# Two pairs of the first batch in two rounded parts from row 256 on, with the first expert unit's product grown chunk by chunk

## The chip, the cores and the metric

The kernel runs on one core of one Trainium2 chip. The metric is the device time of one execution in microseconds (us), as the median of several runs.

The engines are named as in the profile: PE is TensorE (matrix products), PEld its weight loads, DVE is VectorE, ACT is ScalarE, POOL is GpSimd, SP is SyncE, which here only issues DMAs.

## The reference

Inputs: q, k, v of 4 batches x 8 heads x 576 rows x 64, a forget gate f per row, and two pairs of weights (512 x 2048 and 2048 x 512). The output has 2304 rows of 512.

```python
scores = scale * np.matmul(q, k.transpose(0, 1, 3, 2))
cum = np.cumsum(np.log(np.clip(f, 0.0001, 1.0)), axis=-1)
decay = cum[:, :, :, None] - cum[:, :, None, :]
scores = np.where(causal, -1000000000.0, scores + decay)
attn = softmax(scores)                    # over the last axis
x = np.matmul(attn, v)                    # heads side by side: 2304 x 512
h = x @ w_in;  x = np.maximum(h, 0.0) ** 2 @ w_out
h = x @ w2_in; out = np.where(h > 0, h, np.exp(np.minimum(h, 0)) - 1) @ w2_out
```

## The kernel before, in words

**Attention** takes the heads of a batch in pairs, four pairs to a batch. A head's rows come in two parts: part A is rows 0 to 255, part B rows 256 to 511; step 4 takes the last 64 rows of both heads of a pair together. In the first batch all four pairs do part A first (8 steps), and then pair by pair step 4 and two B steps (12 steps); the other batches go pair by pair through all five. A step computes scores on PE (`s`), the row minimum on DVE, the exponential on ACT, transposes the result on PE (`pt`), copies it out of PSUM, and multiplies with v on PE (`pv`). A pair's output is scaled (`r`, `rb`, `pr`) and split for what follows (`xs`, or for the first 256 rows of the first batch `x0`).

**Two ways to multiply.** A head can be *plain*: q, k and v stay 32-bit floats (`rawA`, `rawB`, `rawC`, `vp`), a score is one matmul (L374), and the product with v is one (L453); the profile shows two records for each. Or it is in *two rounded parts*: `load_head` makes of the fetched `raw` a rounded part and the rest (`qk1`, `qk2`, `vv`), a score is two single-record matmuls (L378, L379), and the weights are split into two parts as well (`p`, `ptA`, `ptB`), so that v takes two matmuls (L456). Making the parts takes two ACT copies, one DVE cast and four POOL instructions for a head of the first batch's B part, whose lists `ENG` give the engine of each. In the first batch every part A is plain, and part B of all pairs below `PLAIN_B`, which is 4.

**The first expert layer** begins inside attention: six units of 256 rows multiply with the half of the weights that stays on the chip. A unit runs through `ph` (rows times w_in, four banks `fp` of two columns `fc`, 12 matmuls for each `fc`, 3 for each of its four chunks `c` of 128 inputs), `relu2` (ACT, then a square on ACT or POOL, a rounded copy on ACT and the rest `gl` on POOL), and `o` (times w_out, 96 matmuls). A unit is cut into steps of 12 matmuls. At each place in attention the loop adds credit, `PACE` of the batch times the `COST` of the attention step, and spends it on unit steps. The first unit may start when part A of all four pairs of the first batch is stored. Until then `fill()` has PE multiply zeros (`busy`, tile `idle`).

**Expert weights** come as 64-bit words and are made into floats by `words` (L152 on ACT, L153 to L156 on DVE) and then split (L172 on ACT, L121 on DVE); 16 of them are due in the first batch, at the steps that `W_AT` names. Three of their staging buffers are also the buffers of `qk2`.

A scheduler sets the order of the instructions on each engine from the program's order, from the dependences and from costs of its own; each engine then runs its list in order. The DMAs all go through SP's list.

Of the kernel before, what the change touches and what calls it, by code (L numbers as in the profile page):

```python
# [10 lines left out]
F32 = mybir.dt.float32  # L11
# [8 lines left out]
NC = DM // 128  # L20
# [6 lines left out]
CH = 256  # L27
# [3 lines left out]

W_MIN = float(np.uint32(0x38000000).view(np.float32))
W_MAX = float(np.uint32(0x47EFFE00).view(np.float32))
PACE = (1.4, 0.9, 1.85, 1.75)
COST = {'A': 0.7, '4': 1.1, 'B': 1.7}
W_AT = (1, 1, 1, 1, 0, 0, 0, 0, 2, 2, 2, 2, 2, 2)
AHEAD = 2
# [4 lines left out]

PLAIN = (0,)

PLAIN_B = 4
CP = {'pA': 'a', 'pB': 'av', 'xA': 'a', 'xB': 'a'}
ENG = {'qk': 'aav', 'ql': 'ppp', 'kh': 'pvd', 'kl': 'ppp', 'vh': 'ppp', 'vl': 'ppp', 'xl': 'pv'}
NORM = 'ap'
# [23 lines left out]
def f32(ap):  # L72
    return ap.bitcast(F32)
# [10 lines left out]
def attention_then_moe_kernel(ctx, tc, first, firstv, plain, qkv, aug0, f, w1, w2, out):  # L84
    nc = tc.nc
    PS = bass.MemoryType.PSUM

    def pool(stack, name, bufs, side, **kw):
        return stack.enter_context(tc.tile_pool(name=name, bufs=bufs, side=side, reuse_waits="tile", **kw))
# [25 lines left out]
    trail = []  # L115
# [59 lines left out]
    def win(m, fc, part_, c):  # L175
        return wslot[m, fc][:, part_, c * 128:(c + 1) * 128]

    def wout(m, fc, part_, c=None):
        o = wslot[m, fc][:, part_, 512:1024]
        return o if c is None else o[:, c * 128:(c + 1) * 128]  # L180

    def mm3(dst, pairs, first, last, skip=False):
        n = len(pairs)
        for i, (l, r) in enumerate(pairs):
            nc.tensor.matmul(out=dst, lhsT=l, rhs=r, start=first and i == 0,  # L185
                             stop=last and i == n - 1, skip_group_check=skip)

    def three(hl, hr):
        return [(hl[0], hr[0]), (hl[1], hr[0]), (hl[0], hr[1])]
# [10 lines left out]
    ps_o = pool(un, "ps_o", 1, "left", space=PS)  # L200
    ps_h = pool(un, "ps_h", 1, "left", space=PS)
# [4 lines left out]
    x0 = xa.tile([128, 2 * NC, CH], F32R, tag="xu", name="x0")  # L206
# [44 lines left out]
    zero = const.tile([128, 128], F32R, name="zero")  # L251
    nc.vector.memset(f32(zero), 0.0)
    idle = ps_h.tile([128, 512], F32, tag="h", name="idle")

    def busy(n):
        for _ in range(n):
            nc.tensor.matmul(out=idle[:, 0:256].rearrange("p (a b) -> p a b", a=2), lhsT=zero, rhs=zero.unsqueeze(1).broadcast_to([128, 2, 128]), start=True, stop=True)

    busy(WARM)

    raws = {}
# [3 lines left out]
    def fetch_head(b, h, part):  # L265
        if b in PLAIN and (part == "A" or h // 2 < PLAIN_B):
            fetch_plain(b, h, part)
            return
        raw = ab.tile([128, ALL], F32, tag="raw", name="raw", bufs=BUFS["raw"])
        raws[b, h, part] = raw  # L270
        nc.sync.dma_start(out=raw, in_=qkv[b, h])
# [361 lines left out]
    def load_x1(t0, n, pool):  # L633
        x = pool.tile([128, 2 * NC, n], F32R, tag="xu", name="xu")
        for c in range(NC):
            for off, step, b, s in runs(t0, n):
                nc.sync.dma_start(out=f32(x[:, c::NC, off:off + step]), in_=x1[b][c::NC, :, s:s + step].rearrange("c p t -> p c t"))
        return x

    more = {}  # L640

    def unit(u):
        x = load_x1(u * CH, CH, xa) if u else x0
        if not u:
            nc.sync.dma_start(out=x1[0][:, :, 0:CH].rearrange("c p t -> p c t"), in_=f32(x0))
        yield
        gs = []
        for fp in range(4):
            if more and fp % 2:
                ph = more["h"].tile([128, 512], F32, tag="H", name="ph")  # L650
            else:
                ph = ps_h.tile([128, 512], F32, tag="h", name="ph")
            for i in range(2):
                fc = 2 * fp + i
                for c in range(NC):
                    mm3(ph[:, i * CH:(i + 1) * CH], three([win(1, fc, t, c) for t in range(2)], [x[:, c, :], x[:, NC + c, :]]),
                        c == 0, c == NC - 1)
                if i == 0:
                    yield
            gs += [[t[:, i * CH:(i + 1) * CH] for t in ht] for ht in [relu2(ph, 512, GL[0], SQ[fp])] for i in range(2)]  # L660
            yield
        for cp in range(2):
            if more:
                po = more["o"].tile([128, 512], F32, tag=f"O{cp}", name="o").rearrange("p (c t) -> p c t", c=2)
            else:
                po = ps_o.tile([128, 2, CH], F32, tag="o", name="o")
            for fc in range(8):
                for i in range(2):
                    mm3(po[:, i, :], three([wout(1, fc, t, 2 * cp + i) for t in range(2)], gs[fc]), fc == 0 and i == 0, fc == 7, True)
                if fc % 2:  # L670
                    yield
            o = xa.tile([128, 2, CH], F32, tag="o", name="o")
            if CPO == "v":
                nc.vector.tensor_copy(o, po)
            else:
                nc.scalar.activation(out=o, in_=po, func=AF.Copy)
            nc.sync.dma_start(out=part[u][:, 2 * cp:2 * cp + 2, :], in_=o)
        yield

    def drain(gen):  # L680
        for _ in gen:
            pass
# [39 lines left out]
    def ready(u):  # L722
        b, s = divmod(u * CH + CH - 1, S)
        return stored[b] == 2 * (H // 2) or (b in SPLIT and s < 256 and stored[b] >= H // 2)

    stored = [0] * B
    units = [unit(u) for u in range(NU)]
    started = [False] * NU
    wl = weights(1, w1, wa, range(8), False, True)

    wait = [0]
    n_step = [0]

    def moe_step():
        for u in range(NU):
            if units[u] is None:
                continue
            if not started[u] and not ready(u):
                return False
            if not started[u] and u:  # L740
                if wait[0] < DELAY:
                    wait[0] += 1
                    return False
            started[u] = True
            wait[0] = 0
            n_step[0] += 1
            if n_step[0] == 9:
                drain(wl)
            if HOLD is not None and len(trail) > HOLD:
                with tc.issue_after(trail[-1 - HOLD].ins):  # L750
                    left = next(units[u], "end") != "end"
            else:
                left = next(units[u], "end") != "end"
            if left:
                return True
            units[u] = None
        return False

    credit = 0.0
    for i in range(len(todo) + LAG):  # L760
# [12 lines left out]
        if i < len(todo):  # L773
            sg = soft(*todo[i])
            b, hp, kind, k = todo[i]
        else:
            sg = iter(())
        if i >= LAG:
            o = todo[i - LAG]
            og = outs(*o)  # L780
        else:
            o, og = None, iter(())
        for _ in range(W_AT[i] if i < len(W_AT) else 0):
            next(wl, None)
        n_moe = PACE[b] * COST[kind]
        n_out = {"A": 3, "4": 1, "B": 8}[o[2]] if o else 1
# [52 lines left out]
    while moe_step():  # L839
        pass  # L840
# [358 lines left out]
```

## Time and profile before

| | |
|---|---|
| median of 3 runs | 1034.13 us (1031.56 to 1039.54) |
| the profiled execution | 1034.08 us, of which its span 1032.3 us |
| granted TensorE clock | 0.998 of full speed |
| busy over the span | PE 98%, DVE 69%, ACT 51%, POOL 25% |
| attention | 0 to about 362 us; the rest is the two expert layers |

A row of the timeline gives the start and the length of an instruction or of a run of equal ones; lengths of matmuls overlap, since PE is pipelined, so that the distance of two starts is what one costs PE. The chain that ended last gives lengths that don't overlap.

### The profile page before, as it was taken

How to read it: one execution, taken by the hardware profiler on the slowest of the kernel's cores; microseconds unless marked ns; L12 is line 12 of the kernel's file. 1: busy time of each engine (PE TensorE's matmuls, PEld its weight loads, DVE VectorE, ACT ScalarE, POOL GpSimd, SP SyncE). 2: the span in 40 equal slices, each digit the busy share in tenths (PEclk: the TensorE clock that was granted, in tenths of full speed). 3: DMA queues.
4: the chain of work that ended last, by engine and by line, in shares of the span. 5: the costliest groups of instructions: out<-in, count | busy, mean ns of one | idle time of the engine just before them, and what ended most of it. 6: DMA issues, size and time to landing. Idle time of an engine off the chain costs nothing.

```text
span 1032.3 us, 17606 instructions
## 1 busy us (share of the span) xinstructions
PE 1015.1 (98%) x6385; PEld 901.1 (87%) x6385; DVE 707.2 (69%) x1585; ACT 523.1 (51%) x1195; POOL 258.9 (25%) x280
## 2 busy tenths in 40 slices
PE   8999999999999999999999999999999999999998
PEld 7677798999999998889988888888989898899997
DVE  6994588776685548946385779795555999654554
ACT  5774586766676634424253445463334665433331
POOL 2235588576775300003104040300000000000000
PEclk9999999999999999999999999999999999999999
DMA  6764555554641174333545545644415465453402
GB/s 221 220 204 130 185 165 156 184 164 142 182 130 54 45 249 125 128 123 144 168 138 204 201 166 204 225 153 154 136 49 178 145 209 180 126 177 126 147 21 82
DMA packets 73862, 158.47 MB, mean 154 GB/s; under 512 B 9296, under 2 KB 34640, under 8 KB 73744
## 3 DMA queue, kind: packets, MB, share of 16 engines
q1 hardware_dynamic: 73776, 157.36, 46.9%
q8 instruction: 50, 0.82, 0.3%
q14 instruction: 36, 0.29, 0.1%
HBM read 115.15 MB, written 39.22 MB: 150 GB/s over the span
## 4 chain that ended last, share of the span: by engine, by line
PE 93%; DMA 2%; DVE 2%; SPq 1%; POOL 1%; issue 0%; ACT 0%; DVEq 0%; ACTq 0%; POOLq 0%
PE O L185 32%; PE P L185 18%; PE pH L185 13%; PE ph L185 7%; PE o L185 7%; PE pt L449 5%; PE pv L456 4%; PE s L374 2%; PE pv L453 2%; PE s L378 2%; PE s L379 2%; SPq L281 1%; DMA rawB<-in_qkv_dram 1%; DMA wraw<-in_w_dram 1%; PE pr L449 1%; DMA aug<-in_aug_dram 1%
## 5 line engine op out<-in xcount | busy, mean ns | idle before, releaser
L185 PEld LDWEIGHTS P<-xu,v 128*128 128x128 f32 x1536 | 200.5, 189 | 10.8 <-issue 0.6
L185 PE MATMUL P<-xu,v 128*128 128x256 f32 x1536 | 203.8, 282 | 0.4 <-ACT hs L1040 0.4
L185 PE MATMUL O<-v,gh 128*128 128x512 f32 x576 | 169.2, 393 | 1.8 <-ACT gh L1011 1.8
L185 PE MATMUL pH<-xu,w 128*128 128x512 f32 (+1 forms) x672 | 140.8, 360 | 0.0
L185 PEld LDWEIGHTS pH<-xu,w 128*128 128x128 f32 x672 | 114.0, 188 | 20.2
L185 PE MATMUL O<-gh,w 128*128 128x512 f32 (+1 forms) x448 | 122.6, 362 | 0.0
L185 PEld LDWEIGHTS O<-v,gh 128*128 128x128 f32 x576 | 102.9, 188 | 19.7 <-ACT gh L1011 2.0
L185 PE MATMUL O<-v,gl 128*128 128x512 f32 x288 | 100.9, 393 | 0.0
L185 PEld LDWEIGHTS O<-gh,w 128*128 128x128 f32 x448 | 79.8, 189 | 14.1
L1040 ACT ACTIVATE hs<-P 128x256 f32<-128x256 f32 x128 | 48.1, 381 | 81.9 <-PE P L185 81.3
L134 POOL TENSOR_TENSOR yl<-pr,yh 128x512 fp32r<-128x512 f32 x18 | 25.0, 1389 | 250.8 <-ACT yh L860 171.7
L134 POOL TENSOR_TENSOR qk<-raw,qk 64x704 fp32r<-64x704 f32 (+1 forms) x48 | 76.8, 1601 | 22.3 <-DVE qk L129 10.3
L1043 DVE TENSOR_TENSOR hs<-P,hs 128x256 f32<-128x256 f32 x96 | 40.6, 424 | 59.3 <-PE P L185 57.4
L185 PE MATMUL O<-gl,w 128*128 128x512 f32 (+1 forms) x224 | 80.1, 363 | 0.0
L185 PE MATMUL o<-gh,w 128*128 128x256 f32 x384 | 75.8, 290 | 0.0
L1065 ACT ACTIVATE g<-g 128x512 f32<-128x512 f32 x64 | 40.2, 629 | 54.1 <-DVE g L1057 32.2
L152 ACT ACTIVATE wt<-wraw 128x512 f32<-128x512 f32 x57 | 38.4, 675 | 57.4 <-DMA wraw<-in_w_dram 43.1
L618 ACT ACTIVATE gh<-g 128x512 fp32r<-128x512 f32 (+1 forms) x80 | 46.8, 585 | 38.3 <-DVE g L617 35.2
L185 PE MATMUL ph<-xu,w 128*128 128x256 f32 x480 | 65.8, 287 | 0.2 <-ACT g L613 0.2
L617 DVE TENSOR_TENSOR g<-g 128x512 f32<-128x512 f32 (+1 forms) x56 | 45.4, 812 | 26.5 <-ACT g L613 26.3
L1011 ACT ACTIVATE gh<-g 128x512 fp32r<-128x512 f32 x72 | 45.5, 631 | 35.8 <-DVE g L1066 28.8
L185 PEld LDWEIGHTS O<-v,gl 128*128 128x128 f32 x288 | 52.8, 188 | 9.9
(156 smaller groups left out, 2070.2 us busy)
## 6 DMA issues: line engine op xcount, KB each, us to landing
xu<-x SPq DMA_DIRECT2D x66, 512.0 KB
wraw<-in_w_dram SPq DMA_DIRECT2D x57, 512.0 KB
raw<-in_qkv_dram SPq DMA_DIRECT2D x24, 800.0 KB
x<-yh SPq DMA_DIRECT2D x31, 256.0 KB
x<-yl SPq DMA_DIRECT2D x31, 256.0 KB
x<-xs SPq DMA_DIRECT2D x16, 320.0 KB
xu<-x SPq DMA_DIRECT2D x16, 256.0 KB
raws_w<-in_w_dram SPq DMA_DIRECT2D x7, 512.0 KB
```

The costliest lines, as they stand in the source:

```text
L134: nc.gpsimd.tensor_tensor(out=dst, in0=x, in1=f32(hi), op=ALU.subtract)
L152: nc.scalar.activation(out=f32(t), in_=f32(hi), func=AF.Abs)
L185: nc.tensor.matmul(out=dst, lhsT=l, rhs=r, start=first and i == 0, stop=last and i == n - 1, skip_group_check=skip)
L374: seen[0] = nc.tensor.matmul(out=dst, lhsT=hh.t[0:68, hh.q + q0:hh.q + q0 + 128], rhs=hh.t[0:68, hh.k + j0:hh.k + j0 + n], start=first, st ...
L449: seen[0] = nc.tensor.transpose(dst, src, ident[:, c0:c0 + 128])
L456: seen[0] = nc.tensor.matmul(out=dst, lhsT=hh[2][:, J, :], rhs=hl[i], start=first and i == 0, stop=last and i == 1)
L617: (nc.vector if sq == "v" else nc.gpsimd).tensor_tensor(out=g[:, 0:n], in0=g[:, 0:n], in1=g[:, 0:n], op=ALU.mult)
L618: nc.scalar.activation(out=gh[:, 0:n], in_=g[:, 0:n], func=AF.Copy)
L1011: nc.scalar.activation(out=gh, in_=g, func=AF.Copy)
L1040: nc.scalar.activation(out=o, in_=x, func=AF.Copy)
L1043: nc.vector.tensor_tensor(o, y, x, op=ALU.add)
L1065: nc.scalar.activation(out=gs[i], in_=gs[i], func=AF.Exp)
```

## The change

Three things are changed. `PLAIN_B` goes from 4 to 2, so part B and step 4 of the third and the fourth pair of the first batch (heads 4 to 7) go in two rounded parts. The first unit's products for `fp` 0 and 1 are no longer two whole steps each: `begin` computes chunk `c` of both banks when part A of pair `c` is stored, for the first three chunks (six steps of 6 matmuls); the unit itself adds the fourth chunk. The two banks are then open at the same time, one in `ps_h` and one in `ps_o`, and the zero products go into the open bank `ph` and add nothing to it. And `PACE` of the first batch goes from 1.4 to 1.0, with the step at which the remaining weights are drained moved from 9 to 7, since the unit has two steps less.

```diff
-PACE = (1.4, 0.9, 1.85, 1.75)
+PACE = (1.0, 0.9, 1.85, 1.75)
...
-PLAIN_B = 4
+PLAIN_B = 2
...
+    begun = []
+
     def busy(n):
         for _ in range(n):
-            nc.tensor.matmul(out=idle[:, 0:256].rearrange("p (a b) -> p a b", a=2), lhsT=zero, rhs=zero.unsqueeze(1).broadcast_to([128, 2, 128]), start=True, stop=True)
+            out = (begun[0] if begun else idle)[:, 0:256].rearrange("p (a b) -> p a b", a=2)
+            nc.tensor.matmul(out=out, lhsT=zero, rhs=zero.unsqueeze(1).broadcast_to([128, 2, 128]), start=not begun,
+                             stop=not begun, skip_group_check=bool(begun))
...
+    def grow(fp, cs):
+        ph = begun[fp]
+        for c in cs:
+            for i in range(2):
+                mm3(ph[:, i * CH:(i + 1) * CH], three([win(1, 2 * fp + i, t, c) for t in range(2)], [x0[:, c, :], x0[:, NC + c, :]]),
+                    c == 0 and i == 0, c == NC - 1 and i == 1, True)
+
+    def begin():
+        for c in range(NC - 1):
+            for fp in range(2):
+                while stored[0] <= c:
+                    yield False
+                if c == 0:
+                    begun.append((ps_o if fp else ps_h).tile([128, 512], F32, tag="o" if fp else "h", name="ph"))
+                grow(fp, (c,))
+                yield True
...
         for fp in range(4):
-            if more and fp % 2:
+            if not u and fp < 2:
+                ph = begun[fp]
+                grow(fp, (NC - 1,))
+            elif more and fp % 2:
                 ph = more["h"].tile([128, 512], F32, tag="H", name="ph")
             else:
                 ph = ps_h.tile([128, 512], F32, tag="h", name="ph")
             for i in range(2):
+                if not u and fp < 2:
+                    break
...
+    early = begin()
+
     def moe_step():
+        if not started[0]:
+            with tc.issue_after(trail[-1].ins):
+                went = next(early, None)
+            if went is not None:
+                return went
...
-            if n_step[0] == 9:
+            if n_step[0] == 7:
                 drain(wl)
```

How the order moves is shown at three places. In these lists a name stands with the number that its tile has in that program, L260, L378, L382, L383, L453, L457, L460 and L478 of the changed kernel are L257, L374, L378, L379, L449, L453, L456 and L474 of the one before, and `x_122` is `x0`.

**PE, where part A of the third pair is done**, before the first scores from row 256 on. Before:

```order
L453 MATMUL pv<-ea,rawA 64x128
L257 MATMUL idle<-zero 128x256 x14
L374 MATMUL s<-rawA 128x256 x2
L449 MATMUL pt<-ident,e_1_135 128x128 x3
L374 MATMUL s<-rawA 128x256 x2
L449 MATMUL pr<-ident,rb 128x128 x2
```

After:

```order
L260 MATMUL idle<-zero 128x256 x2
L378 MATMUL s<-rawA 128x256 x2
L453 MATMUL pt<-ident,e_1_135 128x128 x3
L185 MATMUL ph<-x_122,w_0_252 128x256 x2
L185 MATMUL ph<-x_122,w_2_315 128x256
L378 MATMUL s<-rawA 128x256 x2
...
L185 MATMUL ph<-x_122,w_1_274 128x256 x3
L260 MATMUL ph<-zero 128x256 x9
```

The first chunk of the unit's product (12 matmuls) now stands here; the second and third stand behind the first scores from row 256 on, and zero products stand beside them.

**PE, at the first scores of the third pair from row 256 on** (`qk_850` to `qk_904` are the parts of its two heads). Before:

```order
L185 MATMUL ph<-x_122,w_5_565 128x256 x3
L449 MATMUL pt<-ident,e_1_135 128x128
L449 MATMUL pt<-ident,eb 128x128 x2
L374 MATMUL s<-rawB 128x288
L374 MATMUL s<-rawC 128x288
L374 MATMUL s<-rawB 128x288
L374 MATMUL s<-rawC 128x288
L453 MATMUL pv<-pp,rawB 64x320
```

After:

```order
L260 MATMUL ph<-zero 128x256 x2
L185 MATMUL ph<-x_122,w_0_252 128x256 x3
L185 MATMUL ph<-x_122,w_1_274 128x256 x3
...
L185 MATMUL ph<-x_122,w_3_375 128x256 x3
L382 MATMUL s<-qk_850 128x288 x2
L383 MATMUL s<-qk_851 128x288
L382 MATMUL s<-qk_903 128x288
L383 MATMUL s<-qk_851 128x288
L382 MATMUL s<-qk_903 128x288
```

The scores are now single-record matmuls on the prepared parts, and the unit has come to `fc` 3 here, where it had come to `fc` 5.

**POOL, from the end of part A of the first batch on.** Before:

```order
L134 TENSOR_TENSOR x_122<-xA,x_122 128x256 x3
L474 TENSOR_SCALAR r<-zB 128x4
L127 TENSOR_SCALAR rb<-r 128x256
L134 TENSOR_TENSOR gl<-g,gh 128x512
L617 TENSOR_TENSOR g<-g 128x512
L134 TENSOR_TENSOR gl<-g,gh 128x512
```

After:

```order
L127 TENSOR_SCALAR vv<-raw 128x5x64
L478 TENSOR_SCALAR r<-zB 128x4
L134 TENSOR_TENSOR vv<-raw,vv 128x5x64
L127 TENSOR_SCALAR rb<-r 128x256
L134 TENSOR_TENSOR qk_850<-raw,qk_850 64x576
L127 TENSOR_SCALAR vv<-raw 128x5x64
L134 TENSOR_TENSOR vv<-raw,vv 128x5x64
L134 TENSOR_TENSOR qk_903<-raw,qk_903 64x576
L134 TENSOR_TENSOR qk_851<-raw,qk_850 64x448
```

POOL prepares the third pair's heads here; the unit's squares and rests stand behind them, and the fourth pair's and the second batch's heads follow.

## Rows read from the trace of the kernel before

**Rows 1.** Busy time by stretch: from:to, length, each engine's busy us (instructions), clock, DMA.

```profile
41.20:82.00 40.80, 40.80 (x238) 30.27 (x239) 39.41 (x91) 29.42 (x66) 10.60 (x12) 1.00 0.69 201
...
112.60:200.00 87.40, 83.67 (x624) 76.37 (x623) 69.56 (x212) 62.16 (x175) 65.19 (x70) 1.00 0.54 168
125.00:175.00 50.00, 48.65 (x374) 46.17 (x374) 42.91 (x126) 38.18 (x107) 43.33 (x46) 1.00 0.51 159
```

**Rows 2.** The chain that ended last, 39 to 71 us: start, us, what.

```profile
38.98 2.04 DMA rawB<-aug
41.16 2.18 PE s L374 x8
...
53.97 1.42 PE ph L185 x12
55.39 0.86 PE s L374 x2
...
56.58 1.22 PE pv L453 x4
...
62.37 0.58 PE pv L453 x4
...
65.41 0.65 PE s L374 x2
...
70.83 1.94 PE s L374 x8
```

**Rows 3.** The same chain in the second batch, 130 to 143 us.

```profile
130.00 0.14 PE s L379
...
131.41 0.23 PE s L378
...
136.79 0.18 PE s L378
...
141.27 1.25 PE pv L456 x10
```

**Rows 4.** PE's timeline: the second batch's first score.

```profile
112.63 0.28 PE L378 MATMUL s<-qk 128*128 128x256 f32 x1
```

**Rows 5.** DVE's timeline: reductions of the first and third pair; word instructions.

```profile
42.89 0.46 DVE L382 CUSTOM_DVE_ANT_0 e<-s,mz 128x288 f32<-128x288 f32 x1 [0.39 <-PE s L374]
...
51.56 0.42 DVE L154 TENSOR_SCALAR wt<-wt 128x512 int32<-128x512 int32 x1
...
52.50 0.69 DVE L155 SCALAR_TENSOR_TENSOR wt<-wraw,wt 128x512 int32<-128x512 int32 x1
...
55.52 1.52 DVE L154 TENSOR_SCALAR wt<-wt 128x512 int32<-128x512 int32 x1
...
73.54 0.44 DVE L382 CUSTOM_DVE_ANT_0 e<-s,mz 128x288 f32<-128x288 f32 x1
```

**Rows 6.** POOL's timeline: two instructions beside such of rows 5.

```profile
55.50 1.27 POOL L134 TENSOR_TENSOR gl<-g,gh 128x512 fp32r<-128x512 f32 x1 [0.29 <-ACT gh L618]
...
72.90 1.04 POOL L134 TENSOR_TENSOR xs<-xB,xs 128x320 fp32r<-128x320 f32 x1
```

**Rows 7.** POOL's groups in 75 to 125 us: busy us, mean ns of one.

```profile
L134 POOL TENSOR_TENSOR qk<-raw,qk 64x704 fp32r<-64x704 f32 x4 | 6.8, 1710 | 2.0 <-DVE qk L129 2.0
L134 POOL TENSOR_TENSOR qk<-raw,qk 64x576 fp32r<-64x576 f32 x4 | 5.7, 1425 | 0.3
...
L127 POOL TENSOR_SCALAR vv<-raw 128x320 fp32r<-128x320 f32 x3 | 2.6, 854 | 10.1 <-PE pv L453 6.3 <-DMA raw<-in_qkv_dram 3.1 <-PE pr L449 0.7
...
L474 POOL TENSOR_SCALAR r<-zA 128x4 f32<-128x4 f32 x1 | 0.2, 198 | 0.1
```

**Rows 8.** SP's timeline: two DMA issues.

```profile
62.98 0.50 SPq L281 DMA_DIRECT2D rawB<-in_plain_dram  x1
...
81.07 0.42 SPq L271 DMA_DIRECT2D raw<-in_qkv_dram  x1
```

**Rows 9.** DVE's timeline: the first cast of the head that the second issue of rows 8 fetches.

```profile
85.75 0.83 DVE L129 CAST qk<-raw 128x1280 fp32r<-128x1280 f32 x1 [1.26 <-DMA raw<-in_qkv_dram]
```

## The prediction

> **What bounds the kernel now.** I read the busy time by stretch first. From 41.2 us on PE is busy without a gap up to 82 us, and between 112.6 and 200 us it is idle for 87.40 - 83.67 = 3.73 us [rows 1]. Until 41 us nothing of part B can start: the chain comes out of a DMA that ends there, `rawB<-aug` [rows 2], and no row of SP's list up to it is moved by the change. From there the chain is PE. Two engines stand close behind it: DVE is busy for 39.41 of 40.8 us up to 82 us, with the weights' word instructions, and POOL for 43.33 of 50 us from 125 to 175 us [rows 1], with the parts of the second batch's heads. So what PE is spared counts, unless DVE or POOL then comes later than PE does.
>
> **Rounded parts, on PE.** Per head, the plain scores of 512 and 384 columns take 0.86 and 0.65 us, the product with v two times 1.22/2 and, by the same row, a third time 0.61, then 0.58 for the last two pieces: 1.51 + 2.41 us. Per pair step 4 takes 1.94 us [rows 2]. In rounded parts each score is two matmuls, at 0.23 and 0.18 us, so 0.82 us; the product with v takes 1.25 us in all; step 4 takes eight at 0.14, 1.12 us [rows 3]. Four heads save 4 x (1.51 - 0.82) + 4 x (2.41 - 1.25) = 7.4 us, two pairs 2 x (1.94 - 1.12) = 1.6 us: **9.0 us** less for PE.
>
> **The growing product.** No matmul is added or left out. One costs 1.42/12 = 0.12 us [rows 2]. Of the 48 for `fp` 0 and 1 only the first chunk's 12 come to stand ahead of the first scores from row 256 on, in time that PE spends on zero products: 1.4 us gained there. But the unit now counts as not started for longer, so the fills go on: 131 zero products stand in the new list where 113 stood, and behind the 41 us mark 33 instead of 7. The 18 more cost 18 x 0.12 = 2.2 us of PE's total, and this total already has the early 12 in it. Summed over PE's whole list with such prices, the work falls from 1007.2 to 1000.4 us, **by 6.8 us** (9.0 - 2.2).
>
> **1.0 steps.** This removes no work. It lets attention run ahead of the unit: when the second batch's first score stands in the list, 72 of the unit's matmuls, 72 x 0.12 = 8.6 us, are still to come, where before none were. About as many (69) stand at the end of attention, where no engine's waits need them as a cover. The price is zero by itself; the effect is that POOL has less PE time to work under.
>
> **DVE.** From the first reduction of step 4 to that of the third pair it takes 73.54 - 42.89 = 30.65 us [rows 5], all work and waits for POOL. The list now has more in front of the third pair's: three instructions of a weight (0.69 us each and in rows 0.6 apart), two casts of the new heads' k (half of the 0.83 of a cast twice as long [rows 9]) and a copy: 3.5 us, so 77.0 us. PE's list there has 35.8 us of work behind 41.2, and with what it lost to changes of form and waits before, it comes to the next scores at 79. So DVE's delay costs nothing, by some 2 us; if POOL stretches it more, it costs what goes beyond them. The bounds are 0 and 3.5 us; I take 0. ACT's eight copies, net eight more split copies and four folds (some 9 us) lie in a stretch where it is busy for 29.42 of 40.8 us [rows 1]; its share stays under that of the other three.
>
> **POOL and the DMA of the heads.** This is the term that decides. The third pair's second head needs the buffer of the first pair's first, so its DMA is issued at about the place of the `rawB` that waited for this buffer, 62.98 us [rows 8]. A head of 800 KB issued at 81.07 us is first read at 85.75 [rows 8, 9], 4.7 us later: the head is there at **67.7 us**. The first head of the pair comes earlier and doesn't matter. The bounds of this arrival are 66 (an earlier release) and 74 us (the 1.2 MB more in these four transfers, at 201 GB/s [rows 1], all in front of it); I take the rows' value. From there POOL's list goes on without a gap to spare: up to the second head of the third batch it has 86 instructions: 10 of 1.71 us, 13 of 1.43, 22 for `vv` at 0.86, 4 for the 448 columns of q (no row; between 0 and 1.43, by length 1.11), and 37 between 0.2 and 1.3 us (eleven groups, of which the first and the last and two more stand in [rows 7]): 84.6 us. PE's list, if it never waited, comes to this head at 41.2 + 112.1 us of work, and with 3.2 us for changes of form (between 41.16 and the second batch's first score at 112.63 [rows 2, 4] it had 68.3 us of work in 71.5) at **156.5 us**. POOL comes there at 67.7 + 84.6/share. At a share of 1 that is 152.3; at the 43.33/50 = 0.867 of [rows 1] it is 165.3, 8.8 us behind PE. In that row POOL had some lead, and part of its idle time was waiting for buffers that PE held; where POOL is the late one, this part falls away. I take 0.88: 163.8 us, 7.3 us behind. The 3.73 us that PE lost here before are in the old time and not paid again: **3.6 us** to pay.
>
> So the sum is 1034.08 - 6.8 + 3.6 = 1030.9. The profiled execution is within 0.1 us of the median, so I keep its scale: 1031 us.
>
> **Where POOL holds DVE up.** A word instruction of 0.42 us took 1.52 us when it began at 55.52 us, 0.02 us behind a POOL instruction of 1.27 us, and ended 0.3 us after that one; the reduction at 73.54 us, which reads PSUM, took its usual 0.44 us beside a POOL instruction that had begun at 72.90 [rows 5, 6]. Between the third pair's reduction and the second batch's first, the new list has 17.2 us of DVE work and 20 us of POOL's. At the rate of the first stretch (30.65 us for 26.0 us of listed work, beside 10.6 us of POOL [rows 1, 5]: 0.45 us lost per us of POOL) DVE comes there at 77.0 + 17.2 + 9 = 103 us, where PE, at 41.2 + 53.6 + 3.2, comes at 98; if each us of POOL cost one, at 114. Half of the 17.2 us are instructions on PSUM, so I take half the rate, 99 us, which PE's own time covers but for 1 us. The Trainium skill ("SBUF — State Buffer", section "Who interferes with whom") speaks against this change here: of a DVE instruction in the two-port mode and a GpSimd one, the second is blocked for the other's whole length. By that rule alone the sum would be by the 114.
>
> **The rivals.** *POOL keeps up.* If POOL's share is near 1, PE doesn't wait for it, and the 72 matmuls that the unit has left fill the gaps of the second batch: -6.8 - 3.7, so 1023.6 us. For it speaks that PE waits for little there now; against it that POOL has been idle for an eighth of that stretch, and that each head's POOL work begins behind a DVE cast. *POOL gives it all back.* At a share of 0.852 POOL comes at 167.0 us, 10.5 us behind PE, and what is paid is the whole 6.8: 1034. *POOL becomes the bound.* Below 0.852 the change is slower: at 0.80 POOL comes at 173.5 us, 17.0 - 3.7 = 13.3 us are paid, and the time is 1040.6 us. For it speaks that POOL, DVE and the buffers of `qk2` (three) now wait for each other with no lead, against it that the list of PE has unit work spread through that batch. *POOL blocks DVE us for us.* Then the second batch begins at 114 instead of 98 us; the 3.7 us are not paid twice, and the time is 1034.1 - 6.8 + 16 - 3.7 = 1039.6. Against it speaks the reduction that was not stretched. *The growth doesn't do what it says:* 12 matmuls in front of the DMA's end are 1.4 us, and the fills that it prolongs cost 2.2; that is in the sum, and if PE waits for DVE up to 77 us anyway, these fills cost nothing and the time is 1029.
>
> **How the numbers follow.** The forecast, 1027 to 1033, with the case of free fills in it: 0.48. All given back, 1033 to 1036: 0.19. POOL keeps up, 1020 to 1027: 0.20. POOL as the bound, 1036 to 1050: 0.09; DVE blocked us for us, 1036 to 1042: 0.04. The range leaves out the ends of the last three: 1023 to 1040. About 1%, 10 us, is what a measurement of this kernel can tell from no change, since the three runs lie 0.8% apart: faster than 1023.8 has 0.09 (near half of its case), slower than 1044.5 has 0.06 (most of POOL as the bound, whose arrival I know least), and between them 0.85.
>
> **What would show it.** Right: the second batch's first score at 97 to 102 us instead of 112.6; POOL busy for over 85% between 68 and 165 us, and PE's waits there named after POOL's `qk` or DVE's casts, 5 to 10 us in all; attention's end at about 345 to 350 us, since 69 unit matmuls stand behind it; the two expert layers as long as before. Wrong: head 5 landing past 74 us, DVE's third pair past 80, a PE wait for the rest `gl` behind attention, or POOL's share outside 0.82 to 0.95.

## The result, and the profile after

The changed kernel takes **1044.32 us** (median of 8 runs, 1039.8 to 1048.16), the kernel before 1034.51 us (median of 8, 1031.44 to 1039.54). The ratio is **1.0089, 95% interval 1.0072 to 1.0107**: slower, by some 9 us, where 1031 was predicted. The profiled execution took 1045.46 us.

The head of the changed kernel's page, to be held against 1032.3 us of span and 1015.1 us of PE before:

```profile
span 1043.7 us, 17724 instructions
...
PE 1017.1 (97%) x6403; PEld 907.5 (87%) x6403; DVE 721.9 (69%) x1601; ACT 531.4 (51%) x1211; POOL 274.8 (26%) x296
...
PEclk9899999999999999999999999999999999999999
```

PE was to have 6.8 us less to do, and is busy for 2 us longer. To see why, I split each span into three terms that make it up: **work** (PE's busy time at full clock), **idle** (the span less PE's busy time), and **half clock** (what a lower granted clock added: PE's busy time times one less the granted clock, summed over windows of 1 us). Before: 1013.4 + 17.2 + 1.7 us. After: 1008.9 + 26.6 + 8.2. So the change took 4.5 us of work away, and brought 9.4 us of idle time and 6.5 us at half clock: +11.4 in the profiled executions. The last term isn't one execution's accident: the mean granted clock of the 8 runs after is 0.986 to 0.995, median 0.991, against 0.993 to 1.000, median 0.9965, in 26 runs of the kernel before. A span times (1 - clock) gives 9.4 and 3.6 us.

Windows of the changed kernel (columns as in [rows 1]) show where:

```profile
39.00:41.00 2.00, 0.21 (x2) 0.00 (x0) 1.97 (x5) 1.70 (x4) 0.00 (x0) 0.92 0.34 59
41.00:50.00 9.00, 8.72 (x26) 6.42 (x27) 3.75 (x11) 2.46 (x6) 0.72 (x1) 0.50 0.99 293
...
85.00:88.50 3.50, 3.50 (x17) 2.98 (x16) 3.50 (x6) 1.23 (x2) 1.67 (x2) 0.51 0.02 4
75.00:112.00 37.00, 32.62 (x207) 26.69 (x206) 35.17 (x72) 25.30 (x61) 31.03 (x28) 0.95 0.47 151
112.00:200.00 88.00, 81.75 (x626) 77.06 (x625) 71.68 (x213) 63.55 (x180) 69.52 (x76) 1.00 0.60 181
```

The granted clock is 0.50, the 1.2 GHz level, from 41 to 50 us and again from 85 to 88.5 us, each time behind a stretch in which PE stood idle (0.21 of 2 us busy in the first row). In the kernel before it was 1.00 in all of 23 to 400 us. From 75 to 112 us PE is idle for 4.38 us, where before it was busy for all 37; from 112 to 200 us for 6.25 us, before 3.73. DVE is busy for 35.17 of 37 us in the first of these, before for 18.31. But from 41 to 50 us it works for only 3.75 us, before for 8.43: it waits for scores that PE makes at half speed.

The same in PE's timeline after; the second and the third row answer to the 41.16 us row of [rows 2], the last to [rows 4]:

```profile
38.34 0.86 PE L457 MATMUL pv<-e,rawA 128*64 128x256 f32 x4
41.27 2.26 PE L378 MATMUL s<-rawB 68*128 68x288 f32 x4 [2.07 <-DMA rawB<-aug]
43.33 2.13 PE L378 MATMUL s<-rawC 68*128 68x288 f32 x4
...
80.34 0.38 PE L453 MATMUL pt<-ident,eb 128*128 128x128 f32 x2
83.42 0.50 PE L383 MATMUL s<-qk 68*128 68x288 f32 x2 [2.70 <-DVE qk L129]
...
109.07 0.28 PE L382 MATMUL s<-qk 128*128 128x256 f32 x1
```

The DMA ends where it did before, but PE has nothing between 39.2 and 41.27 us, and the eight scores behind it take 4.2 us (2.18 in [rows 2]). The third pair's scores wait 2.70 us for a DVE cast. DVE's timeline after shows that cast (79.27 us), an undisturbed one of the same size (72.09), a third one (87.64), two instructions of the weights, and the reductions that answer to [rows 5]:

```profile
44.53 0.46 DVE L386 CUSTOM_DVE_ANT_0 e<-s,mz 128x288 f32<-128x288 f32 x1 [3.41 <-PE s L378]
...
72.09 0.45 DVE L129 CAST qk<-qk 64x576 fp32r<-64x576 f32 x1
...
73.38 1.68 DVE L153 TENSOR_SCALAR wt<-wt 128x512 f32<-128x512 f32 x1 [0.37 <-ACT wt L152]
74.98 1.65 DVE L121 TENSOR_TENSOR w<-wt,w 128x512 fp32r<-128x512 f32 x1
...
79.27 4.05 DVE L129 CAST qk<-qk 64x576 fp32r<-64x576 f32 x1
...
87.27 0.45 DVE L386 CUSTOM_DVE_ANT_0 e<-s,mz 128x288 f32<-128x288 f32 x1
...
87.64 2.49 DVE L129 CAST qk<-qk 64x576 fp32r<-64x576 f32 x1
```

And POOL's beside it:

```profile
71.76 0.46 POOL L127 TENSOR_SCALAR vv<-raw 128x320 fp32r<-128x320 f32 x1 [9.92 <-DMA raw<-in_qkv_dram]
72.30 0.97 POOL L134 TENSOR_TENSOR vv<-raw,vv 128x320 fp32r<-128x320 f32 x1
73.35 2.72 POOL L134 TENSOR_TENSOR qk<-raw,qk 64x576 fp32r<-64x576 f32 x2
...
78.92 1.44 POOL L134 TENSOR_TENSOR qk<-raw,qk 64x448 fp32r<-64x448 f32 x1
80.33 1.03 POOL L621 TENSOR_TENSOR g<-g 128x512 f32<-128x512 f32 x1
81.32 1.26 POOL L134 TENSOR_TENSOR gl<-g,gh 128x512 fp32r<-128x512 f32 x1
82.56 0.45 POOL L127 TENSOR_SCALAR vv<-raw 128x320 fp32r<-128x320 f32 x1
...
87.42 1.15 POOL L134 TENSOR_TENSOR qk<-raw,qk 64x448 fp32r<-64x448 f32 x1 [1.83 <-DVE wt L156]
88.53 1.28 POOL L134 TENSOR_TENSOR gl<-g,gh 128x512 fp32r<-128x512 f32 x1
```

The cast of 0.45 us took 4.05 us beside a chain of POOL instructions without a gap, and ended 0.3 us behind the four from 78.92 on; the third cast took 2.49 us and ended 0.3 us behind POOL's two from 87.42 on. The two instructions of the weights (0.42 and 0.68 us undisturbed) took 1.68 and 1.65 us beside POOL's of 73.35. The Trainium skill ("SBUF — State Buffer", section "Who interferes with whom") says that one of two such instructions blocks the other for its whole length; these rows agree with it, over chains of four and of two.

Windows from the first pair's reduction to the third's, first of the kernel before, then of the changed one:

```profile
42.89:73.54 30.65, 30.65 (x172) 21.95 (x171) 29.98 (x71) 23.50 (x53) 8.53 (x10) 1.00 0.83 242
```

```profile
44.53:87.27 42.74, 40.04 (x204) 27.30 (x203) 38.72 (x79) 27.62 (x61) 17.12 (x18) 0.90 0.57 194
```

DVE takes 12.1 us longer: 8.7 us more of busy time and 3.4 us more of idle time (4.02, before 0.67), 2.4 us of which is waiting for scores.

### The profile page after: what moved, and what is told of

The parts are those of the page before. It is cut to its first block, busy times and chain, and to the rows that moved or that the text cites. A ratio compares the mean times of both kernels' runs of the same rounds, so it can differ in the third digit from the quotient of the medians.

```text
span 1043.7 us, 17724 instructions
## 1 busy us (share of the span) xinstructions
PE 1017.1 (97%) x6403; PEld 907.5 (87%) x6403; DVE 721.9 (69%) x1601; ACT 531.4 (51%) x1211; POOL 274.8 (26%) x296
## 4 chain that ended last, share of the span: by engine, by line
PE 85%; DMA 6%; DVE 5%; ACT 2%; issue 1%; SPq 1%; POOL 0%; ACTq 0%; DVEq 0%
PE O L185 32%; PE P L185 17%; PE pH L185 13%; PE o L185 6%; PE ph L185 5%; PE pv L460 3%; PE pt L453 3%; DMA raw<-in_qkv_dram 2%; DMA x<-xs 2%; PE s L382 1%; PE s L383 1%; PE s L378 1%; DMA xu<-x 1%; DVE qk L129 1%; DMA rawB<-in_qkv_dram 1%
## 5 line engine op out<-in xcount | busy, mean ns | idle before, releaser
L134 POOL TENSOR_TENSOR qk<-raw,qk 64x576 fp32r<-64x576 f32 (+2 forms) x56 | 87.9, 1569 | 23.7 <-DVE qk L129 8.6
L185 PEld LDWEIGHTS ph<-xu,w 128*128 128x128 f32 x480 | 60.6, 190 | 0.8 <-DMA xu<-x 0.8
```

The costliest lines, as they stand in the source:

```text
L134: nc.gpsimd.tensor_tensor(out=dst, in0=x, in1=f32(hi), op=ALU.subtract)
```

## The experiments

The edits change the program that a scheduler orders anew, so that most of them also move other instructions. The table has every run with the three terms of its profiled execution; R, G and P are the parts of the change (rounded parts, growing product, 1.0 steps). The profiled execution isn't always near the median. The ratio (with its interval) is that of all runs, to runs of the kernel before that were made beside them, so it isn't the quotient of two medians in this table.

| kernel | parts | median us | ratio | span | work | idle | half clock |
|---|---|---|---|---|---|---|---|
| before | - | 1034.5 | 1 | 1032.3 | 1013.4 | 17.2 | 1.7 |
| after | R G P | 1044.3 | 1.0089 (1.0072 to 1.0107) | 1043.7 | 1008.9 | 26.6 | 8.2 |
| e5_round | R | 1040.8 | 1.0042 (1.0023 to 1.0062) | 1035.0 | 1003.4 | 26.5 | 5.1 |
| e6_grow | G | 1035.8 | 1.0009 (0.9993 to 1.0024) | 1035.1 | 1012.0 | 18.4 | 4.7 |
| e7_pace | P | 1043.5 | 1.0075 (1.0051 to 1.0099) | 1040.2 | 1014.9 | 20.2 | 5.1 |
| e8_round_grow | R G | 1041.0 | 1.0044 (1.0026 to 1.0063) | 1039.1 | 1004.3 | 26.8 | 8.0 |
| e9_round_pace | R P | 1056.2 | 1.0209 (1.0191 to 1.0226) | 1054.2 | 1009.5 | 33.2 | 11.5 |
| e4_plain | G P | 1053.0 | 1.0167 (1.0133 to 1.0202) | 1051.5 | 1018.0 | 23.6 | 9.9 |
| e1_full | R G P + edit | 1050.4 | 1.0142 (1.0113 to 1.0170) | 1049.5 | 1008.7 | 27.7 | 13.1 |
| e2_kh_act | R G P + edit | 1043.0 | 1.0078 (1.0053 to 1.0103) | 1047.5 | 1009.2 | 28.0 | 10.3 |
| e3_both | R G P + edit | 1051.9 | 1.0168 (1.0143 to 1.0193) | 1049.4 | 1007.4 | 29.4 | 12.6 |
| e10_round_nopool | R + edit | 1038.4 | 1.0031 (1.0013 to 1.0049) | 1034.9 | 1005.6 | 24.2 | 5.1 |
| e11_nopool | R G P + edit | 1048.5 | 1.0131 (1.0108 to 1.0155) | 1045.4 | 1007.4 | 29.5 | 8.5 |
| e12_early14 | R G P + edit | 1039.8 | 1.0050 (1.0031 to 1.0070) | 1037.4 | 1003.8 | 25.8 | 7.8 |
| e13_early14_nopool | R G P + edits | 1035.8 | 0.9986 (0.9961 to 1.0011) | 1031.9 | 1004.7 | 20.5 | 6.7 |
| e14_pool_load | - + edit | 1041.7 | 1.0071 (1.0051 to 1.0092) | 1038.9 | 1014.1 | 19.9 | 4.9 |
| e15_late_w | R G P + edits | 1036.6 | 1.0015 (1.0005 to 1.0025) | 1036.3 | 1003.8 | 22.9 | 9.7 |
| e16_last_pair | half of R | 1042.0 | 1.0062 (1.0040 to 1.0085) | 1040.5 | 1009.4 | 26.1 | 5.0 |
| e17_grow_nopool | R G + edit | 1030.3 | 0.9948 (0.9925 to 0.9971) | 1027.4 | 1003.9 | 21.8 | 1.7 |
| e18_v_pool | R G P + edits | 1040.8 | 1.0054 (1.0033 to 1.0075) | 1041.7 | 1004.5 | 26.2 | 11.0 |

**First round: one cause at a time.** *e1_full* puts four zero products ahead of the first scores from row 256 on and holds these scores behind them:

```
+        if i == 8:
+            with tc.issue_after(avs[11].ins):
+                busy(4)
+            with tc.issue_after(zeros[-1].ins):
+                drain(sg)
         drain(sg)
```

> The changed kernel with the idle time ahead of the first scores from row 256 on filled: the product of head 6 with v, the growing product's second chunk and four zero products now stand in front of these scores on PE, not behind. Theory C (the clock): the granted clock is 1.0 from 40 to 55 us (0.50 from 40 to 50 in the changed kernel), the four scores on rawB take 1.2 us, not 2.26, and the time falls by 4.4 us (8.8 us of work at half speed) and up to 1.6 us of idle time that is now used: 1038 to 1040. Theory D (DVE and POOL behind it): PE comes earlier to the third pair's second head but the cast of its k still ends at 83 us, so PE's wait there grows from 2.7 us to 7 or 8 and the time stays at 1043 to 1044.

It came out at 1.0142, slower than the changed kernel: neither theory. The clock held at 40 us, but PE's list was 2.6 us late by then (head 5's product with v at 40.95 us, not 38.34), and the scores, which now have to wait for what stands in front of them, came at 44.66; then the clock fell from 53 to 61, from 91 to 98 and twice later. As a test of the clock at 40 us it is inconclusive.

*e2_kh_act* moves the casts of the rounded parts' k from DVE to ACT:

```
-'kh': 'pvd'
+'kh': 'pad'
```

> The changed kernel with the copies of k in the rounded parts (64x576, four of them) on ACT, not on DVE. Theory D: PE's wait of 2.70 us for the cast at 80.6 us goes, with it the fall of the clock from 85 to 88.5 us (some 1.7 us), and DVE is 5 us less late: 1039 to 1041. Theory C (the fall at 40 us is what counts; DVE is late only because PE was): the wait for the cast is replaced by another wait of about that length for DVE's reductions; 1042 to 1044. The clock from 40 to 50 us stays at 0.50 by both.

1.0078 against 1.0089: no change that shows. The wait for the cast is gone, but PE now waits 2.1 us for a copy by DVE before 112 us and 2.9 us for another instruction of DVE's behind it. That is theory C's half of the expectation: the cast was the place where DVE's lateness showed, not its cause.

*e3_both* is the two edits together:

> Both edits, of e1_full and e2_kh_act, at once. If the two causes are separate, their gains add: 1034 to 1036. If DVE is what PE waits for in either case, e1's gain shows only here: 1034 to 1036 with e1 alone at 1043. If neither: 1040 or more, and the loss lies in the second and third batch (6.3 us of idle PE between 120 and 200 us, 3.7 before).

1.0168: as with e1_full, nothing gained; of no use for the split.

*e4_plain* undoes the rounded parts (`PLAIN_B = 4`):

> The changed kernel with the rounded parts undone (all four pairs plain from row 256 on); the growing product and the 1.0 steps stay. PE's list up to 57 us is the same. Theory C: the clock still falls at 40 us; PE has 9.0 us more work but no cast to wait for; 1034.5 + 4.4 (clock) + 1.2 (idle) + 0.8 (zero products less early matmuls) = 1040 to 1042. Theory D (the rounded parts' work on DVE and POOL is the cause): 1034 to 1036.

1.0167, far above both expectations. PE's timeline of it shows the wait and the slow scores of the changed kernel, with no rounded part in the program:

```profile
38.68 0.86 PE L457 MATMUL pv<-e,rawA 128*64 128x256 f32 x4
41.75 2.26 PE L378 MATMUL s<-rawB 68*128 68x288 f32 x4 [2.20 <-DMA rawB<-aug]
```

So the fall at 40 us (4.8 us here as there) doesn't need the rounded parts, and the rounded parts are worth 8.7 us to the changed kernel (1053.0 - 1044.3), near the 9.0 us of work that they save.

**Second round: each part alone.** The edits are `PLAIN_B = 2`; the code of the growing product; `PACE = (1.0, ...)`; and the changed kernel with `PACE = (1.4, ...)`. The moved drain goes with the growing product in these runs.

> The kernel before with the rounded parts alone: pairs 3 and 4 in two rounded parts, no growing product, 1.4 steps. e4_plain showed that undoing the rounded parts in the changed kernel costs 9 us. Theory R (the 9.0 us of PE work count in full wherever they stand): 1025 to 1028. Theory D (the casts and POOL's parts of these heads make PE wait, here as in the changed kernel, 4.4 us of idle time and 1.7 of clock between 75 and 112 us, and the kernel before has none there): 1031 to 1034.

> The kernel before with the growing product alone (1.4 steps, all pairs plain). Theory G (the zero products that it displaces ahead of the first scores from row 256 on let the clock fall at 40 us): clock 0.50 from 40 to 50 us, 4.8 us lost there and up to 1.5 us for idle time and zero products: 1039 to 1042. Theory P (the loss comes with the 1.0 steps): 1033 to 1036, clock 1.0 from 40 us on.

> The kernel before with 1.0 steps alone. Theory P (the unit's matmuls no longer cover PE's waits in the second batch, nor at attention's end, and the clock falls there: in e4_plain 4.3 us more than before between 112 and 200 us and 3.2 us more between 300 and 400): 1041 to 1043. Theory G: 1034 to 1036.

> The changed kernel with the steps back at 1.4: rounded parts and growing product. Theory G: the fall of the clock at 40 us and the waits of the changed kernel stay, 1040 to 1044. Theory P: the second batch's waits (6.3 us between 112 and 200 us) and those after 300 us (1.5) go, and the 9.0 us of the rounded parts show: 1030 to 1035. Both: 1035 to 1038.

*e5_round*: 1.0042, above both. The work falls by 10.0 us (9.0 predicted), and 9.3 us of idle time and 3.4 at half clock take it back: theory D's direction, and more of it than expected. *e6_grow*: 1.0009, theory P's value; the clock doesn't fall at 40 us. *e7_pace*: 1.0075, theory P's value and half a us more, though not for its reasons alone: of its 8 us, 3.0 are idle time (2.9 of it between 112 and 200 us), 1.5 work and 3.4 half clock, half of that in the first 41 us, half behind a wait at 678 us, where 1.0 steps change nothing. *e8_round_grow*: 1.0044, theory G's value by the median (1041.0 us), but with half of its reason: without 1.0 steps no fall at 40 us, but 5.4 us of idle time and 4.6 at half clock between 75 and 112 us.

*e9_round_pace* completed the eight combinations later:

> Rounded parts with 1.0 steps, no growing product. If the effects of the parts of the change simply add (rounded parts alone 1.0042, 1.0 steps alone 1.0075): 1046 to 1048. If 1.0 steps need the rounded parts (with the growing product, taking them away cost 9 us in e4_plain): 1034 to 1037.

1.0209, more than the sum. The parts don't add: beside R and P the growing product gains 12 us, beside P alone it costs 9.5.

**Third round: POOL, and the place of the fills.** In *e10*, *e11* and *e13* nothing of the rounded parts is prepared on POOL:

```
-ENG = {..., 'ql': 'ppp', 'kh': 'pvd', 'kl': 'ppp', 'vh': 'ppp', 'vl': 'ppp', ...}
+ENG = {..., 'ql': 'pvp', 'kh': 'pad', 'kl': 'pvp', 'vh': 'pap', 'vl': 'pvp', ...}
```

and in *e12* and *e13* the first eight entries, all ahead of row 256, go at 1.4 steps, which puts the growing product's first matmuls and the zero products where e6_grow had them:

```
-        n_moe = PACE[b] * COST[kind]
+        n_moe = (1.4 if i < 8 else PACE[b]) * COST[kind]
```

> The rounded parts alone (as e5_round, which measured 1.0042 of before), but none of their preparation on POOL: the three differences of a head on DVE, the copies of its k and v on ACT (of k it was DVE). POOL loses 16 instructions and 17 us, DVE gets 12 instructions and 6 us for 4 casts less (2 us unstretched). Theory B (DVE's instructions between SBUF tiles are held up while POOL works, so the parts on POOL make DVE late): DVE's word instructions go back to 0.42 and 0.68 us, PE's idle time between 75 and 112 us falls from 3.9 us to under 1, no fall of the clock there; 1029 to 1034. Theory L (DVE's list is just too long there): DVE has 4 us more to do, PE waits longer; 1042 to 1046.

> The changed kernel with the same move of the rounded parts' preparation from POOL to DVE and ACT. Theory B: the idle time of 4.4 us and the 1.7 us of clock between 75 and 112 us go; the fall at 40 us stays: 1037 to 1040. Theory L: 1046 to 1050.

> The changed kernel with 1.4 steps for the first eight entries, 1.0 from the first scores of row 256 on: the growing product's 12 first matmuls and the zero products stand ahead of these scores as in e6_grow, where the clock did not fall at 40 us. Theory C (what stands in the last 5 us before these scores decides on the clock there): 1.0 from 40 to 55 us, 4.8 us of the loss gone; DVE's lateness at 80 us stays or grows: 1038 to 1041. If the fall at 40 us is caused otherwise: 1043 to 1045.

> The changed kernel with both edits, of e11_nopool and e12_early14. Theories B and C together: none of the two falls of the clock, PE idle only in the second batch as in the changed kernel; 6.8 us less work and 2.5 us more idle time than before: 1029 to 1033. If one of them is wrong: 1037 to 1041; if both: 1043 or more.

*e12_early14* came out as theory C has it: 1039.8. Windows of it:

```profile
36.00:41.00 5.00, 4.22 (x29) 3.26 (x28) 4.84 (x10) 3.99 (x11) 2.05 (x3) 1.00 0.37 130
41.00:50.00 9.00, 9.00 (x49) 6.12 (x48) 8.90 (x21) 5.33 (x11) 0.99 (x1) 1.00 0.94 269
```

PE is busy up to the scores, the clock stays at 1.00 (2.4 GHz), and DVE has its 8.90 us of work between 41 and 50 us instead of 3.75. The lateness at 80 us stays, with a fall from 76 to 82.5, and another comes from 137 to 144. It is 4.6 us faster than the changed kernel, but not by the clock: by the table, half clock goes only from 8.2 to 7.8 us, and work falls by 5.1 us, of which 23 instructions less on PE (6380, after 6403) at 0.12 us are 2.8. The mean clock of its runs (median 0.990) is no higher than that of the changed kernel's (0.991). So the run shows an order that held the clock at 40 us, and not that the time depends on it.

*e10* gains 2.4 us on e5_round, with intervals that overlap: not shown, and between its two theories. *e13* gains 4.0 us on e12 (5.3 us less idle time) and ends level with the kernel before, above its expectation: the clock falls at three other places (71.6, 146.6 and 167 us). *e11* is 4.1 us slower than the changed kernel, theory L's value. Its waits of PE between 75 and 112 us begin with:

```profile
PE s L382 <- DVE qk L121: 3.9, 1, 3.9
```

That is one of the differences that I had moved to DVE. With the fall at 40 us, DVE begins its list late, and whatever is put on it comes later still; without the fall (e13, and e17 below) there is room. This is read from the rows; no run changed it alone.

**Fourth round: POOL alone, DVE alone.**

```
+        if 9 <= i <= 16:
+            with tc.issue_after(seen[0].ins):
+                for _ in range(6):
+                    less(zero, mz[:, 0:128], zero)
         drain(sg)
```

> The kernel before with 48 extra subtractions on POOL (128x128, in groups of six from the first scores of row 256 on; nobody reads them): about 17 us of POOL work, as much as the rounded parts bring, and nothing else. The order on PE and DVE is that of the kernel before. Theory B (POOL's work holds DVE's instructions between SBUF tiles up): the words' instructions stretch to 1.0 to 1.6 us between 45 and 85 us, DVE comes 5 us or more later to the third and fourth pair's reductions, PE waits and the clock falls once: 1038 to 1044. If POOL's work holds nobody up: 1034 to 1036.

1.0071, **theory B's value**, and the cleanest of these runs: on PE, DVE, ACT and SP the order of instructions is that of the kernel before. DVE's timeline of it:

```profile
68.37 1.27 DVE L154 TENSOR_SCALAR wt<-wt 128x512 int32<-128x512 int32 x1
...
71.81 1.76 DVE L156 SCALAR_TENSOR_TENSOR wt<-wraw,wt 128x512 int32<-128x512 int32 x1
...
80.44 0.44 DVE L382 CUSTOM_DVE_ANT_0 e<-s,mz 128x288 f32<-128x288 f32 x1
...
84.41 1.38 DVE L154 TENSOR_SCALAR wt<-wt 128x512 int32<-128x512 int32 x1
```

The third pair's reduction comes at 80.44 us instead of 73.54 [rows 5]; the first came 1.4 us later as well, ahead of the first subtraction (45.03 us), so 5.5 us were added between the two. The window between them, to be held against the first of the two windows above:

```profile
44.31:80.44 36.13, 33.30 (x179) 23.18 (x178) 32.98 (x73) 24.45 (x52) 32.80 (x47) 0.95 0.68 194
```

POOL has 24.3 us more in it (32.80, before 8.53), so that each us of POOL cost 0.23 us. Of the 5.5 us, 3.0 are busy time of DVE (32.98, before 29.98), instructions that took longer; 2.5 are idle time, of which 1.8 is waiting for POOL's own `r`, which stood behind the subtractions. So POOL makes DVE late in two ways. The load is also heavier than was expected: POOL is busy for 291.5 us, 32.6 more than before and not 17, where the rounded parts alone add 17.6 (e5_round). That POOL's work can do it is shown; the rounded parts' price is not these 7 us. PE is then idle for 2.3 us between 75 and 112 us, and the clock falls once behind 41 us, from 76 to 81.

> e13_early14_nopool with the weights' words of the second layer spread over eight entries (one each), not four (two each). Theory L (DVE's list between 41 and 112 us is what PE waits for): PE's idle time between 41 and 112 us, 4.4 us there, and the fall of the clock at 71 us go: 1029 to 1033. If PE's waits there are ACT's or POOL's, or the words come too late for the unit's second product: 1035 to 1039.

`W_AT` ends `2, 2, 1, 1, 1, 1, 1, 1, 1, 1` instead of six times `2`. 1.0015, theory L's expectation missed: a shorter list on DVE gains nothing, and PE still waits 3.3 us there for a reduction.

> The kernel before with rounded parts for the last pair alone. PE is spared about half, 5 us. Theory B with L (the preparation costs only where DVE has no room: up to 82 us it is full with the weights' words, from there to 112 us it is busy for half of the time): 1030 to 1033. If the preparation costs wherever it stands, half of what the two pairs cost in e5_round: 1036 to 1038.

1.0062, no cheaper than both pairs (1.0042; the intervals overlap) and far from both expectations: 8.9 us more idle time for 4.0 us less work. PE waits 2.6 us for a DVE copy before 112 us, and 6.4 us between 112 and 200 us (2.0 of it for two DMAs). So the prediction's sum fails even where DVE and POOL seemed free; why half of the parts costs as much as all of them isn't settled.

**Last round: can it gain?** *e17* is e8_round_grow with the preparation off POOL; *e18* is e13 with the copies of v back on POOL (`'vh': 'ppp'`).

> Rounded parts with their preparation on DVE and ACT, growing product, 1.4 steps throughout: e8_round_grow (1.0044 of before) without POOL's part. Theory B: of the 5.4 us of idle time and 4.6 us of clock that e8_round_grow has between 75 and 112 us, most goes: 1030 to 1035, and the 1.0 steps add nothing. If without the 1.0 steps the move helps no more than in e10_round_nopool (2 us): 1038 to 1040.

> e13_early14_nopool with the copies of v (128x320, four, some 0.45 us each) back on POOL. In e13_early14_nopool PE waited 1.6 us for an ACT copy of the unit near 70 us, and the clock fell behind it (1.6 us lost). If ACT's four more copies caused that: 1031 to 1034. If it is the unit's own chain: 1035 to 1038.

*e17_grow_nopool* came out as theory B has it, **faster than both kernels: 1030.3 us, 0.9948 (0.9925 to 0.9971)**, 10.7 us less than e8_round_grow. Windows of it:

```profile
75.00:112.00 37.00, 33.90 (x236) 29.33 (x235) 33.17 (x87) 28.73 (x72) 18.94 (x20) 1.00 0.59 177
112.00:200.00 88.00, 82.00 (x633) 77.77 (x633) 71.63 (x212) 63.74 (x179) 69.25 (x76) 1.00 0.56 178
```

Its idle time is still 4.6 us above that of the kernel before, but no wait between 41 and 400 us is longer than 1.4 us, and from 24 to 1026 us the clock doesn't fall (1.00 in both rows). So its 9.5 us less work show, less the idle time. *e18_v_pool* missed: 1.0054, 5 us slower than e13 for four copies of 0.45 us. Its clock falls at 91, 125, 155 and 176 us, behind waits of up to 2.9 us; a scheduler's new order lies between the two kernels, so I don't put that down to the copies.

## Why the prediction was wrong

- *PE's work.* 6.8 us less predicted, 4.5 measured. The zero products aren't the miss: 131 ran, as listed. The rounded parts alone took 10.0 us away (9.0 predicted). 1.0 steps, whose price I had put at zero, added 1.5 alone (e7_pace), and 6.1 beside the rounded parts with no instruction more on PE (e9_round_pace against e5_round, 6385 in both); what that is made of stays open.
- *"So DVE's delay costs nothing."* This step failed. I had DVE at the third pair's reduction at 77.0 us and PE at 79; DVE came at 87.27, and PE waited for its cast up to 83.42. Of the 10.3 us, 1.6 stand ahead of the first pair's reduction (44.53, before 42.89), 3.4 are more idle time behind it, most of it waiting for scores, and 5.2 are the 8.7 us of busy time less the 3.5 that I had listed: instructions that took longer beside POOL (the cast alone 3.6). It cost 4.4 us of idle time up to 112 us, and a fall of the clock. That POOL's work can make DVE and PE late is shown by e14_pool_load. How much of the 4.4 us is POOL's isn't: its removal gained in e17 against e8 and in e13 against e12, where the order of other instructions moved too, lost 4.1 us in e11 against the changed kernel, and in e10 against e5 no gain shows.
- *The half rate for POOL and DVE* (0.22 us lost per us of POOL). Over the stretch of e14_pool_load it was 0.23, waits for POOL's `r` included; but in the cast that PE waited for it was us for us, and an average doesn't show that. I forecast the second batch's first score at 97 to 102 us; it came at 109.07. The rival "POOL blocks DVE us for us", 1039.6 us at a chance of 0.04, had the mechanism of that cast.
- *POOL as the term that decides.* POOL first read head 5 at 71.76 us (67.7 predicted, within 66 to 74), but PE's waits between 112 and 400 us bear DVE's name (4.2 us for reductions, 1.9 for split copies) and not POOL's `qk`, and POOL's share from 68 to 165 us is 77.01/97 = 0.79, outside my 0.82 to 0.95. That the size was near (2.5 us more idle time between 112 and 200 us, where I had 3.6) is chance, since the waits were others. Another 1.3 us came between 200 and 400 us, where I had none.
- *The growing product costs next to nothing.* True alone (e6_grow). *1.0 steps have no price*: false; alone they cost 8 us, 0.75% of the time.
- *The clock stood in no term.* Every product that I moved was priced at full clock, the zero products ahead of 41 us too: "in time that PE spends on zero products: 1.4 us gained". The new places of these matmuls left PE idle for the last 2.07 us ahead of the scores, and 8.72 us of its busy time behind it ran at half clock. With the second fall this is 6.5 us, the largest term of the miss and more than the whole forecast's distance from no change. That the place of the fills matters for the clock there is shown by e12_early14; its gain in time is that of work. It isn't the list alone: in e9_round_pace, with the zero products of the kernel before and a wait of 1.08 us, the clock also fell, from 41 to 44.8 us.
- *Attention's end* was predicted at 345 to 350 us; the last score is at 350.45.

The profiled execution took 14.6 us more than the sum (1045.5 and 1030.9): 2.3 of work, 4.4 of idle time up to 112 us, 1.3 between 200 and 400, 6.5 at half clock and 1.2 elsewhere, less the 1.1 that the second batch's waits cost less than forecast.

What stays open: why the parts combine as they do (R P 1056, R G P 1044; e16 no cheaper than e5). In these kernels waits of 1 to 4 us fall into other places, and a fall follows some of them and not others; I didn't find a rule by which they could have been counted beforehand.

## What to carry to other kernels

Price a change on the engine that you relieve only after asking what prepares its operands: here 10 us less work on TensorE put some 17 us on GpSimd, which can hold up VectorE (5.5 us for 24 us more of GpSimd in e14_pool_load), and TensorE then waited for VectorE. With the preparation on VectorE and ScalarE one kernel was faster than before (e17_grow_nopool), and four were not (e10, e11, e13, e15). Look at filler instructions as part of the schedule: what is moved out of or into a gap ahead of a wait can decide whether the work behind runs at full clock, and a wait that lets the clock fall costs its own length and half of the time until it rises. Read the mean granted clock of every run beside its time: span times (1 - clock) is the part of the time that no list of instructions shows.

## What the runs showed of the hardware

The same wait may let the clock fall or not. In the expert layers PE waits for ScalarE, in the kernel before for 1.83 us and in e7_pace for 1.88 us. The row behind that wait and a window from 0.5 us later on, first of the kernel before:

```profile
672.50 2.11 PE L185 MATMUL O<-v,gh 128*128 128x512 f32 x8 [1.83 <-ACT gh L1011]
```

```profile
673.00:677.00 4.00, 4.00 (x25) 3.52 (x25) 2.85 (x8) 2.81 (x7) 0.00 (x0) 1.00 0.52 195
```

and of e7_pace:

```profile
679.50 3.34 PE L185 MATMUL O<-v,gh 128*128 128x512 f32 x8 [1.88 <-ACT gh L1011]
```

```profile
680.00:684.00 4.00, 4.00 (x16) 3.32 (x15) 2.81 (x8) 2.62 (x7) 0.00 (x0) 0.57 0.53 196
```

25 matmuls in one, 16 in the other; this alone is 1.7 us. It fell at this place in e2_kh_act and e9_round_pace as well. The spread of a kernel's own runs goes with such falls: the mean clock of the kernel before goes from 0.993 (1040.2 us) to 1.000 (1032.4 us). The falls came behind waits of 1.0 us (e2_kh_act, at 40 us) to 4.0 us (e12_early14, at 137 us), and lasted 3 to 10 us. From 41 to 50 us the scores of 1.21 us took 2.26. The Trainium skill ("TensorE: Matmul & The Clock Gate", section "HAM oscillation — how this bites in real kernels") tells of a loss of half of the time spent at the lower level, over and above the wait. These scores agree with it.

A VectorE instruction beside GpSimd took nine times its length here (0.45 us and 4.05 us for the same cast), where GpSimd's instructions followed each other without a gap; a reduction out of PSUM beside GpSimd kept its 0.44 us (e14_pool_load, 80.44 us).
